# Keys and values of a linear attention: values as weights, both signs' features moving, feature sums on VectorE

## The chip, the cores and the metric

The kernel runs on one core of one Trainium2 chip. The metric is the device time of one execution in microseconds (us). A core has a matrix engine (TensorE, called PE in the profile; its weight loads are PEld), a vector engine (VectorE, DVE), an activation engine (ScalarE, ACT), GpSimd (POOL), and a queue engine (SyncE, SP) that issues most DMA transfers. Matrix products read SBUF, the working memory of 128 partitions, and write PSUM, the accumulation memory of eight banks.

## What is computed

The reference normalizes `x` (2048 tokens, 1024 columns) and feeds it to two parts. One is a linear attention with 32 heads of 32 columns, the other a gated feed-forward of width 3584. The result is `x + attention * silu(feed-forward)`. The attention is what the change touches:

```
phi_k = concat(softmax(k @ w_phi), softmax(-(k @ w_phi)))     # 64 features per token and head
kv  = einsum("bhsf,bhsd->bhfd", phi_k, v)                     # per head: 64 features x 32 value columns, summed over tokens
z   = einsum("bhsf->bhf", phi_k)                              # per head: 64 sums over tokens
num = einsum("bhqf,bhfd->bhqd", phi_q, kv)
den = einsum("bhqf,bhf->bhq", phi_q, z) + 1e-6
o   = num / den
```

So there are 32 features of the positive sign and 32 of the negative for each head, and two sums over the 2048 tokens: `kv` and `z`.

## The kernel before

The large products are made with a Strassen-Winograd scheme of seven block products (the table `ORDER`), in three passes of a split into two 32-bit parts, and each block product is 12 matmuls of 128x128 by 128x512. The stages follow one another: gate and up projections of the feed-forward (about 20 to 1117 us), keys and values (to about 1455), queries (to about 1611), the down projection (to about 2150), and attention output with the output projection (to the end).

In the stage of keys and values `heads` (line 921) runs 16 times: for each half of the heads (`c` 0 and 1, 16 heads each) over eight pairs of token tiles of 128 tokens. One call makes the seven block products (L930), which give keys (already multiplied by `w_phi`) and values of two token tiles. ScalarE and VectorE take them out of PSUM: keys of the first tile after product A12 (L938), values after S2, S1, S3 and S4 (L947 to L955), keys of the second tile after A22.

`keys` (line 898) calls `features` (line 106), which makes the softmax of both signs for one tile: per head the largest and smallest key (L110, L111), the two differences (L112, L113), the exponential on ScalarE (L115), the sums over 32 features (L118), the reciprocal (L119), the product with it (L121). The result is `ev`, 128 tokens by 1024: 512 columns of the positive sign, 512 of the negative. `room_e` (line 889) gives it a place. There are three in turn: two lie in large tiles `rooms_ev` of 2048 columns, where the features have the first 1024, and the values of the tile (`room_v`, line 883) have columns from 1024 on. The third consists of two separate tiles of 512 columns from the pool `work`, tag `h1`, so that its exponential, sums and product are two instructions each.

`kv` (line 902) adds one tile to `kv` and `z` in PSUM. The 512 columns of each sign are taken in groups of four heads: 8 groups `m` by 4 heads `h`, 32 calls. Each call has the 32 features of one head and sign as weights (128 tokens by 32) and moves the head's 32 value columns and two columns of ones (34). So column 32 of the result is `z`. The four heads of a group go to four groups of 32 partitions of the result and to four column groups of the matrix engine. A call on 32-bit data becomes two instructions with two weight loads. `kv_run` (line 912) does this for the two tiles of the previous call of `heads`, between the products S2 and S1 of the present one: 128 instructions of L907. For the last pair, two runs of one tile each are made.

After each half `kv_out` (line 1100) takes the result out: ScalarE copies the `kv` columns, VectorE takes the `z` columns (and adds 1e-6 for the positive sign) into 128x8, PE transposes that (L1111), ScalarE copies it, and SP stores both to DRAM (L1115 to L1118), from where the last stage loads them (`load_z`, `load_kvs`).

In this stage only PE's order is that of the program (`in_order(ENG.PE)`, line 1192). The order on the other engines and queues is set at build time by a planner with estimated durations. In the queries' last part all engines have the program's order again. Operands of `x` (`reload`, line 625) come through the pool `q` of 11 buffers of 512 KB, seven for each pair of tiles; SP issues these loads, the loads of the weights, and the split of `wo` that runs alongside (`wo_split`, line 1181).

Of the kernel before, what the change touches and what calls it, by code (L numbers as in the profile page):

```python
# [8 lines left out]
F = mybir.dt.float32  # L9
# [7 lines left out]
S, D, H, DH, FF = 2048, 1024, 32, 32, 3584  # L17
P = 128
# [10 lines left out]
def tile_kernel(ctx: ExitStack, tc: tile.TileContext, x, wkT, wqT, wv, wphi, wo, w1, w3, w2, out):  # L29
    nc = tc.nc  # L30
    open_pools = {}

    def pool(name, bufs, **kw):

        open_pools[name] = tc.tile_pool(name=name, bufs=bufs, reuse_waits="tile", **kw)
        return open_pools[name].__enter__()
# [47 lines left out]
    z_d = dram.tile([2, 2, 4, 4 * DH], F, name="z_d")  # L84
# [21 lines left out]
    def features(e, whole, p):  # L106

        mm = small.tile([P, 2, 16], F, name="mm2")
        p3 = p.rearrange("p (h f) -> p h f", f=DH)
        nc.vector.tensor_reduce(mm[:, 0, :], p3, axis=AX.X, op=OP.max)  # L110
        nc.vector.tensor_reduce(mm[:, 1, :], p3, axis=AX.X, op=OP.min)  # L111
        nc.vector.tensor_sub(heads_of(e[0]), p3, mm[:, 0, :].unsqueeze(2).to_broadcast([P, 16, DH]))  # L112
        nc.vector.tensor_sub(heads_of(e[1]), mm[:, 1, :].unsqueeze(2).to_broadcast([P, 16, DH]), p3)  # L113
        for part in whole:
            nc.scalar.activation(part, part, AF.Exp)  # L115
        r, n = small.tile([P, H], F, name="r"), H // len(whole)
        for k, part in enumerate(whole):
            nc.vector.tensor_reduce(r[:, n * k:n * k + n], heads_of(part), axis=AX.X, op=OP.add)  # L118
        nc.vector.reciprocal(r, r)  # L119
        for k, part in enumerate(whole):  # L120
            nc.vector.tensor_mul(heads_of(part), heads_of(part), r[:, n * k:n * k + n].unsqueeze(2).to_broadcast([P, n, DH]))  # L121
# [18 lines left out]
    small = pool("small", 2)  # L140
    work = pool("work", 5)
# [5 lines left out]
    ps = pool("ps2", 2, space=PSUM)  # L147
# [25 lines left out]
    def quad(name, dt=R):  # L173
        return qp.tile([P, 2, 4, P], dt, name=name, tag="q")
# [7 lines left out]
    ident = misc.tile([P, P], F, name="ident")  # L182
    consts = misc.tile([P, P], F, name="consts")
# [209 lines left out]
    for tb in range(2):  # L393
        for f in range(NF):
# [11 lines left out]
            first = tb == 0 and f < 2  # L406
# [379 lines left out]
    _, sd = rstd(mvs[0], sds[0], casts)  # L786
# [93 lines left out]
    rooms_ev = [rwp.tile([P, 2048], F, name="ev", tag="rw") for _ in range(2)]  # L880
    rooms_at = [0]

    def room_v(k):
        return rooms_ev[k][:, 1024:1024 + 16 * (DH + 2)].rearrange("p (h d) -> p h d", d=DH + 2)

    for k in range(2):
        nc.gpsimd.memset(room_v(k)[:, :, DH:], 1.0)

    def room_e():
        k = rooms_at[0] % 3  # L890
        rooms_at[0] += 1
        if k < 2:
            e = rooms_ev[k][:, :1024]
            return [e[:, :512], e[:, 512:]], [e]
        e = [work.tile([P, 512], F, name="ev", tag="h1", bufs=2) for _ in range(2)]
        return e, e

    def keys(p, e):
        features(*e, p)
        return e[0]  # L900

    def kv(pkv, first, last, e, v):

        for m in range(8):
            for h in range(4):
                sl = slice(32 * h, 32 * h + 32)
                nc.tensor.matmul(pkv[sl, m], e[m // 4][:, (m % 4) * P + 32 * h:(m % 4) * P + 32 * h + 32],  # L907
                                 v[:, 4 * (m % 4) + h], start=first and m == 0, stop=last, skip_group_check=True)

    pkv, out_now = None, []  # L910

    def kv_run(first, last, tiles):

        nonlocal pkv
        if first:
            pkv = ps.tile([P, 512], F, name="pkv", tag="kv", bufs=1)[:, :8 * (DH + 2)]
            pkv = pkv.rearrange("p (h d) -> p h d", d=DH + 2)
        for n, (e, v) in enumerate(tiles):
            kv(pkv, first and n == 0, last and n + 1 == len(tiles), e, v)

    def heads(first, last, apart, xo, wb, steps, pend):

        bank = {}
        for b, an, bn in ORDER:
            if b not in bank:
                bank[b] = ps.tile([P, 512], F, name=f"bank{b}", tag=f"bk{b}", bufs=BANKS[b])
            n = 0
            for k in range(4):
                for u, w in PASSES:
                    nc.tensor.matmul(bank[b], xo[an][:, u, k], wb[bn][:, w, k], start=an in ("A11", "A12", "S1") and n == 0,  # L930
                                     stop=LAST[b] == an and n == 11, skip_group_check=True)
                    n += 1
            pb, pv = bank[b], bank[b].rearrange("p (h d) -> p h d", d=DH)
            if an == "A11":
                k0 = work.tile([P, 512], F, name="k0", tag="w")
                nc.scalar.copy(k0, pb)
            elif an == "A12":
                nc.vector.tensor_add(k0, pb, k0)  # L938
                e0 = keys(k0, room_e())
            elif an == "S2":  # L940
                if pend:
                    kv_run(*pend)
                    if first:
                        out_now.extend(kv_out(0, pkv))
                v0 = room_v(0)
                d0 = v0[:, :, :DH]
                nc.scalar.copy(d0, pv)  # L947
            elif an == "S1":
                v1 = room_v(1)
                d1 = v1[:, :, :DH]  # L950
                nc.scalar.copy(d1, pv)
            elif an == "S3":
                nc.vector.tensor_add(d1, pv, d1)
            elif an == "S4":
                nc.vector.tensor_add(d0, pv, d0)  # L955
            else:
                if apart:
                    kv_run(first, False, [(e0, v0)])
                    e0 = v0 = d0 = None
                    rooms_ev[0] = None  # L960
                e1 = keys(pb, room_e())
            next(steps)
            if out_now and not first:
                out_now.pop()()
        return (False, last, [(e1, v1)]) if apart else (first, last, [(e0, v0), (e1, v1)])
# [97 lines left out]
    def query_heads(i, first, xo, wb, steps):  # L1063

        bank, rho = {}, small.tile([P, 2, 2, 16], F, name="rho")
        for b, an, bn in ORDER:
# [32 lines left out]

    def kv_out(c, pkv):  # L1100
        kvz = work.tile([P, 512], F, name="kvz", tag="w")
        kva, zt = kvz[:, :8 * DH], kvz[:8, 8 * DH:8 * DH + P]
        zs = small.tile([P, 8], F, name="zs")
        nc.scalar.copy(kva.rearrange("p (m d) -> p m d", d=DH), pkv[:, :, :DH])

        nc.vector.tensor_scalar_add(zs[:, :4], pkv[:, :4, DH], 1e-6)
        nc.vector.tensor_copy(zs[:, 4:], pkv[:, 4:, DH])

        def turned():
            pz = ps.tile([P, 512], F, name="pz", tag="kv", bufs=1)  # L1110
            nc.tensor.transpose(pz[:8, :P], zs, ident)  # L1111
            nc.scalar.copy(zt, pz[:8, :P])

        def store():
            nc.sync.dma_start(kv_d[:, :, :, c].rearrange("j f s m d -> (j f) s (m d)"),  # L1115
                              kva.rearrange("p (s n) -> p s n", s=2))
            for s in range(2):
                nc.sync.dma_start(z_d[s, c], zt[4 * s:4 * s + 4])  # L1118

        return [store, turned]  # L1120

# [55 lines left out]
    ps = pool("ps", 2, space=PSUM)  # L1177
# [16 lines left out]
    for c in range(3):  # L1194
        wbn, last = {}, c == 2
# [257 lines left out]
    old, banks, first, second = None, {}, ready[0], None  # L1453
# [3 lines left out]
    for r, new in enumerate(steps):  # L1457
# [29 lines left out]
        for m, (b, an, bn) in enumerate(TURN):  # L1487
# [30 lines left out]
    ps = pool("ps4", 3, space=PSUM)  # L1518
# [54 lines left out]
    for t in range(NT):  # L1573
        p, last = out_half(t, 0), t + 1 == NT
# [70 lines left out]
```

## Time and profile before

| what | value |
|---|---|
| median of 3 runs | 2367.42 us (2367.08 to 2367.56) |
| the profiled execution's own time | 2366.58 us |
| its span, from first to last instruction | 2364.8 us |
| mean granted clock of TensorE | 0.996 |
| PE, DVE, ACT, POOL busy | 99%, 75%, 38%, 11% of the span |

A row of the timeline gives the start in us from the span's start, the length in us, the engine, the line of the kernel, the operation, `out<-in` by the names of tiles, shapes, how many instructions are merged in the row, and in brackets how long the engine was idle before it and what ended that. A row of grouped instructions ends with busy time and mean duration in ns, then idle time before them. An instruction of PE lasts longer than the distance to the next, since they are pipelined; distances between starts tell what PE is held for.

### The profile page before, as it was taken

Reading aid. Unit: us, or ns where it says so; the run is one execution under the profiler, and the core shown is the slowest. Engines: PE = TensorE matmul, PEld = TensorE weight load, DVE = VectorE, ACT = ScalarE, POOL = GpSimd, SP = SyncE. Lnnn points to the kernel's source line nnn. Section 1 sums busy time; section 2 is a strip of 40 time slices with the busy share of each in tenths; the row PEclk is TensorE's granted clock in tenths of the full one; section 3 lists DMA queues with packets and bytes.
Section 4 is the critical chain, followed back from the end, with each engine's and each line's share of the span. In section 5 each row is a group of like instructions: output and inputs, shape, how many; then the busy total and the mean of one; then the engine's idle time right before and its main releaser. Section 6 shows DMA issues by size and latency. Waiting matters only on the chain.

```text
span 2364.8 us, 37648 instructions
## 1 busy us (share of the span) xinstructions
PE 2338.3 (99%) x14640; PEld 1916.5 (81%) x14640; DVE 1777.7 (75%) x2809; ACT 892.8 (38%) x1575; POOL 256.8 (11%) x213
## 2 busy tenths in 40 slices
PE   8999999999999999999999999999999999999999
PEld 6788877788888888888788888787888888888887
DVE  8877788875688888874566666777678888786775
ACT  6445444443355554443221222334433333352000
POOL 1000000000000000000000000331012222213562
PEclk9999999999999999999999999999999999999999
DMA  3556799997788988875978868986444553479763
GB/s 127 162 190 231 241 312 369 344 310 230 241 273 304 305 293 301 288 259 191 365 275 298 305 231 329 362 299 232 161 134 143 205 178 134 156 248 278 211 178 104
DMA packets 301490, 579.08 MB, mean 245 GB/s; under 512 B 24432, under 2 KB 156672, under 8 KB 298624
## 3 DMA queue, kind: packets, MB, share of 16 engines
q1 hardware_dynamic: 294976, 553.60, 69.3%
q10 hardware_dynamic: 6336, 23.07, 2.5%
q8 instruction: 115, 1.88, 0.3%
q14 instruction: 63, 0.52, 0.1%
HBM read 373.69 MB, written 202.91 MB: 244 GB/s over the span
## 4 chain that ended last, share of the span: by engine, by line
PE 95%; DMA 3%; DVE 1%; ACT 1%; issue 0%; SPq 0%; ACTq 0%
PE bankb L667 25%; PE bankb L1400 13%; PE bankc L667 12%; PE pm L1554 8%; PE bankb L930 7%; PE bankc L1400 6%; PE banka L667 6%; PE bankc L930 3%; PE bankb L1004 3%; PE banka L1400 3%; PE bankc L1004 2%; PE banka L930 2%; PE po L1539 1%; DMA xoA<-xo_d0A 1%; PE pkv L907 1%; PE banka L1004 1%
## 5 line engine op out<-in xcount | busy, mean ns | idle before, releaser
L94 DVE TENSOR_TENSOR bo<-rw,bo 128x512 fp32r<-128x512 f32 x329 | 226.1, 688 | 145.3 <-ACT bo L93 145.1
L1400 PE MATMUL bankb<-bo,as 128*128 128x512 f32 x960 | 236.3, 391 | 0.0
L1400 PEld LDWEIGHTS bankb<-bo,as 128*128 128x128 f32 x960 | 181.1, 189 | 37.7
L93 ACT CAST bo<-rw 128x512 fp32r<-128x512 f32 x329 | 202.3, 618 | 19.3 <-ACT wkvo L93 2.9
L667 PE MATMUL bankb<-op0S,bo 128*128 128x512 f32 x672 | 165.7, 396 | 4.5 <-ACT u L703 2.8
L667 PE MATMUL bankc<-op0S,bo 128*128 128x512 f32 x672 | 162.1, 390 | 0.0
L667 PE MATMUL bankb<-op1S,bo 128*128 128x512 f32 x672 | 161.3, 389 | 0.0
L667 PE MATMUL bankc<-op1S,bo 128*128 128x512 f32 x672 | 161.3, 389 | 0.0
L667 PE MATMUL bankb<-op0A,bo 128*128 128x512 f32 x672 | 159.3, 391 | 1.2 <-ACT op0A L765 0.8
L1554 PE MATMUL pm<-wos,oT 128*128 128x512 f32 x672 | 160.0, 393 | 0.0
L1400 PE MATMUL bankc<-bo,as 128*128 128x512 f32 x624 | 158.4, 389 | 0.0
L667 PE MATMUL bankb<-op1A,bo 128*128 128x512 f32 x672 | 157.9, 390 | 0.0
L667 PEld LDWEIGHTS bankb<-op0S,bo 128*128 128x128 f32 x672 | 125.6, 189 | 37.1 <-issue 5.3
L667 PEld LDWEIGHTS bankb<-op1A,bo 128*128 128x128 f32 x672 | 125.8, 188 | 28.1 <-DVE u L711 2.1
L667 PEld LDWEIGHTS bankb<-op0A,bo 128*128 128x128 f32 x672 | 125.4, 188 | 27.6 <-ACT op0A L765 1.1
L667 PEld LDWEIGHTS bankc<-op0S,bo 128*128 128x128 f32 x672 | 125.6, 188 | 27.3 <-issue 1.2
L667 PEld LDWEIGHTS bankc<-op1S,bo 128*128 128x128 f32 x672 | 126.2, 188 | 26.2
L667 PEld LDWEIGHTS bankb<-op1S,bo 128*128 128x128 f32 x672 | 126.2, 188 | 26.2
L1554 PEld LDWEIGHTS pm<-wos,oT 128*128 128x128 f32 x672 | 124.8, 188 | 27.4 <-DVE oT L1545 0.3
L1400 PEld LDWEIGHTS bankc<-bo,as 128*128 128x128 f32 x624 | 117.2, 188 | 24.4
L1414 DVE TENSOR_TENSOR acc<-bankb,acc 128x512 f32<-128x512 f32 x152 | 102.0, 685 | 32.7 <-PE bankb L1400 32.7
L718 ACT ACTIVATE h<-bankb 128x512 f32<-128x512 f32 x56 | 33.5, 598 | 239.7 <-PE bankb L667 239.5
(290 smaller groups left out, 4305.3 us busy)
## 6 DMA issues: line engine op xcount, KB each, us to landing
rw<-in_w SPq DMA_DIRECT2D x112, 512.0 KB, 4.9
hr<-h_d SPq DMA_DIRECT2D x56, 512.0 KB, 4.7
h_d<-h SPq DMA_DIRECT2D x108, 256.0 KB, 5.6
xoS<-xo_d0S SPq DMA_DIRECT2D x44, 512.0 KB, 7.2
xoS<-xo_d1S SPq DMA_DIRECT2D x44, 512.0 KB, 6.7
xoA<-xo_d0A SPq DMA_DIRECT2D x33, 512.0 KB, 5.3
xoA<-xo_d1A SPq DMA_DIRECT2D x33, 512.0 KB, 5.3
e_d<-eq ACTq DMA_DIRECT2D x32, 512.0 KB, 6.5
```

Of the source, the lines that this page charges most:

```text
L93: nc.scalar.copy(hi, src)
L94: (by or nc.vector).tensor_sub(lo, src, hi.bitcast(F))
L667: nc.tensor.matmul(bank[b], bos[tb, f][bn][:, w, k], ao[an][:, u, k], start=first and n == 0, stop=LAST[b] == an and n == 11, skip_group_c ...
L718: nc.scalar.activation(h1, bank["b"], AF.Silu)
L907: nc.tensor.matmul(pkv[sl, m], e[m // 4][:, (m % 4) * P + 32 * h:(m % 4) * P + 32 * h + 32], v[:, 4 * (m % 4) + h], start=first and m == 0 ...
L930: nc.tensor.matmul(bank[b], xo[an][:, u, k], wb[bn][:, w, k], start=an in ("A11", "A12", "S1") and n == 0, stop=LAST[b] == an and n == 11, ...
L1004: nc.tensor.matmul(bank[b], xo[an][:, u, k], wb[bn][:, w, k], start=an in ("A11", "A12", "S1") and n == 0, stop=LAST[b] == an and n == 11, ...
L1400: nc.tensor.matmul(bank[b], t[:, u, pos + k], bos[kb, bn, k][:, w], start=first and n == 0, stop=LAST[b] == an and n == 5, skip_group_chec ...
L1414: nc.vector.tensor_add(c, pb, c)
L1539: nc.tensor.matmul(po[32 * j:32 * j + 32, a, 64 * k:64 * k + 64], kvs[sl, j, c, k], et[sl, :, 4 * k + j], start=True, stop=True, skip_grou ...
L1554: nc.tensor.matmul(p, oTs[t, h][:, a, k], wos[c, 4 * h + k][:, b], start=n == 0, stop=n == 3 * ND - 1)
```

## The change

Weights and moving data of the small products change places. Per head one call now has the 32 value columns as weights and moves the head's 64 features, both signs at once; so a tile takes 16 calls. The result of a head has values on the partitions, and two block transposes on VectorE in `kv_out` turn it. The columns of ones next to the values go. `z` is formed on VectorE: `z_add`, called in `kv_run` for every tile, adds the tile's 1024 features to a running sum of two tiles of 128x512 (the first tile's features are kept in place and added with the second's). At the end of each half, four matmuls with a 128x32 matrix of ones, 256 columns each, sum it over the 128 partitions, and VectorE takes the result out of PSUM. Those two running sums take the two `work` tiles of tag `h1`, and the third place for features becomes a tile of the pool `q`, held for the stage and as wide as the other two. `z` is stored by four small transfers in place of two.

```
     def room_v(k):
-        return rooms_ev[k][:, 1024:1024 + 16 * (DH + 2)].rearrange("p (h d) -> p h d", d=DH + 2)
-
-    for k in range(2):
-        nc.gpsimd.memset(room_v(k)[:, :, DH:], 1.0)
+        return rooms_ev[k][:, 1024:1536].rearrange("p (h d) -> p h d", d=DH)
+
+    ones = consts[:, 64:96]
+    nc.gpsimd.memset(ones, 1.0)
 
     def room_e():
         k = rooms_at[0] % 3
         rooms_at[0] += 1
-        if k < 2:
-            e = rooms_ev[k][:, :1024]
-            return [e[:, :512], e[:, 512:]], [e]
-        e = [work.tile([P, 512], F, name="ev", tag="h1", bufs=2) for _ in range(2)]
-        return e, e
+        if k == len(rooms_ev):
+            rooms_ev.append(quad("ev", F).rearrange("p u k t -> p (u k t)"))
+        e = rooms_ev[k][:, :1024]
+        return [e[:, :512], e[:, 512:]], [e]
...
     def kv(pkv, first, last, e, v):
 
-        for m in range(8):
+        e = e.rearrange("p (s h f) -> p s h f", s=2, f=DH)
+        for m in range(4):
             for h in range(4):
                 sl = slice(32 * h, 32 * h + 32)
-                nc.tensor.matmul(pkv[sl, m], e[m // 4][:, (m % 4) * P + 32 * h:(m % 4) * P + 32 * h + 32],
-                                 v[:, 4 * (m % 4) + h], start=first and m == 0, stop=last, skip_group_check=True)
+                nc.tensor.matmul(pkv[sl, m], v[:, 4 * m + h], e[:, :, 4 * m + h],
+                                 start=first and m == 0, stop=last, skip_group_check=True)
+
+    zsum = []
+
+    def z_add(e):
+
+        if not zsum:
+            zsum.append(e)
+            return
+        if len(zsum) == 1:
+            zsum.extend(work.tile([P, 512], F, name="zsum", tag="h1", bufs=2) for _ in range(2))
+        for n in range(2):
+            half = slice(512 * n, 512 * n + 512)
+            nc.vector.tensor_add(zsum[1 + n], zsum[0][:, half] if zsum[0] is not None else zsum[1 + n], e[:, half])
+        zsum[0] = None
...
         for n, (e, v) in enumerate(tiles):
+            z_add(e)
             kv(pkv, first and n == 0, last and n + 1 == len(tiles), e, v)
...
     def kv_out(c, pkv):
         kvz = work.tile([P, 512], F, name="kvz", tag="w")
-        kva, zt = kvz[:, :8 * DH], kvz[:8, 8 * DH:8 * DH + P]
-        zs = small.tile([P, 8], F, name="zs")
-        nc.scalar.copy(kva.rearrange("p (m d) -> p m d", d=DH), pkv[:, :, :DH])
-
-        nc.vector.tensor_scalar_add(zs[:, :4], pkv[:, :4, DH], 1e-6)
-        nc.vector.tensor_copy(zs[:, 4:], pkv[:, 4:, DH])
+        kva, zt, zs = kvz[:, :8 * DH], kvz[:, 8 * DH:], zsum[1:]
+        zsum.clear()
+        for n in range(2):
+            nc.vector.transpose(kva[:, P * n:P * n + P].rearrange("p (m d) -> p m d", d=DH), pkv[:, :, DH * n:DH * n + DH])
 
         def turned():
             pz = ps.tile([P, 512], F, name="pz", tag="kv", bufs=1)
-            nc.tensor.transpose(pz[:8, :P], zs, ident)
-            nc.scalar.copy(zt, pz[:8, :P])
+            for n in range(4):
+                nc.tensor.matmul(pz[32 * n:32 * n + 32, :256], ones, zs[n // 2][:, n % 2 * 256:n % 2 * 256 + 256],
+                                 start=True, stop=True, skip_group_check=True)
+            nc.vector.tensor_scalar_add(zt[:64], pz[:64, :256], 1e-6)
+            nc.vector.tensor_copy(zt[64:], pz[64:, :256])
```

More of the change, by code (lines that the diff above doesn't have):

```diff
@@ L915, in kv_run @@
         if first:
-            pkv = ps.tile([P, 512], F, name="pkv", tag="kv", bufs=1)[:, :8 * (DH + 2)]
-            pkv = pkv.rearrange("p (h d) -> p h d", d=DH + 2)
+            pkv = ps.tile([P, 512], F, name="pkv", tag="kv", bufs=1)[:, :512 // 2]
+            pkv = pkv.rearrange("p (m n) -> p m n", m=4)
+            zsum.clear()
         for n, (e, v) in enumerate(tiles):
+            z_add(e)
             kv(pkv, first and n == 0, last and n + 1 == len(tiles), e, v)
@@ L945, in heads @@
                 v0 = room_v(0)
-                d0 = v0[:, :, :DH]
+                d0 = v0
                 nc.scalar.copy(d0, pv)
@@ L949, in heads @@
                 v1 = room_v(1)
-                d1 = v1[:, :, :DH]
+                d1 = v1
                 nc.scalar.copy(d1, pv)
@@ L1101, in kv_out @@
         kvz = work.tile([P, 512], F, name="kvz", tag="w")
-        kva, zt = kvz[:, :8 * DH], kvz[:8, 8 * DH:8 * DH + P]
-        zs = small.tile([P, 8], F, name="zs")
-        nc.scalar.copy(kva.rearrange("p (m d) -> p m d", d=DH), pkv[:, :, :DH])
-        nc.vector.tensor_scalar_add(zs[:, :4], pkv[:, :4, DH], 1e-6)
-        nc.vector.tensor_copy(zs[:, 4:], pkv[:, 4:, DH])
+        kva, zt, zs = kvz[:, :8 * DH], kvz[:, 8 * DH:], zsum[1:]
+        zsum.clear()
+        for n in range(2):
+            nc.vector.transpose(kva[:, P * n:P * n + P].rearrange("p (m d) -> p m d", d=DH), pkv[:, :, DH * n:DH * n + DH])
         def turned():
             pz = ps.tile([P, 512], F, name="pz", tag="kv", bufs=1)
-            nc.tensor.transpose(pz[:8, :P], zs, ident)
-            nc.scalar.copy(zt, pz[:8, :P])
+            for n in range(4):
[3 more added lines that the diff above has]
+            nc.vector.tensor_copy(zt[64:], pz[64:, :256])
         def store():
@@ L1116, in store @@
                               kva.rearrange("p (s n) -> p s n", s=2))
-            for s in range(2):
-                nc.sync.dma_start(z_d[s, c], zt[4 * s:4 * s + 4])
+            for n in range(4):
+                nc.sync.dma_start(z_d[n // 2, c].rearrange("(a g) n -> a (g n)", a=2)[n % 2:n % 2 + 1], zt[32 * n:32 * n + 1])
         return [store, turned]
```

2 lines of the change are left out of this document (1 added, 1 removed).

## The prediction

> **What bounds the kernel now.** I read the page first: its busy lines and the chain by engine.
>
> ```profile
> span 2364.8 us, 37648 instructions
> PE 2338.3 (99%) x14640; PEld 1916.5 (81%) x14640; DVE 1777.7 (75%) x2809; ACT 892.8 (38%) x1575; POOL 256.8 (11%) x213
> PE 95%; DMA 3%; DVE 1%; ACT 1%; issue 0%; SPq 0%; ACTq 0%
> ```
>
> TensorE (PE) is busy for 99% of the span and is 95% of the chain that ended last. The edit sits in the key and value stage, so the windows view of that stage comes next.
>
> ```profile
> core 0: us, PE busy (x) PEld busy (x) DVE busy (x) ACT busy (x) POOL busy (x), PEclk, DMA share, GB/s
> 1139.25:1453.00 313.75, 312.80 (x3184) 256.99 (x3185) 196.31 (x293) 66.87 (x103) 0.00 (x0) 0.99 0.81 288
> ```
>
> PE idles 0.95 us of 313.75 there and VectorE (DVE) is busy 196.31, or 63%. GpSimd is not used. So a microsecond is gained or lost here by what PE itself executes, or by a wait that does not exist today. One period of PE, from the timeline of PE alone:
>
> ```profile
> 1360.48 1.37 PE L907 MATMUL pkv<-ev 128*32 128x34 f32 x128
> 1361.78 3.02 PE L930 MATMUL bankc<-op3T,xoS 128*128 128x512 f32 x12
> 1372.80 2.88 PE L930 MATMUL bankb<-op3B,xoA 128*128 128x512 f32 x12
> 1375.52 2.88 PE L930 MATMUL banka<-op3B,xoA 128*128 128x512 f32 x12
> 1378.24 2.88 PE L930 MATMUL bankb<-op3T,xoS 128*128 128x512 f32 x12
> 1381.05 1.34 PE L907 MATMUL pkv<-ev 128*32 128x34 f32 x128
> 1382.40 3.00 PE L930 MATMUL bankc<-op3T,xoS 128*128 128x512 f32 x12
> ```
>
> A product starts every 2.72 us (1372.80, 1375.52, 1378.24). The run of 128 small matmuls on L907 holds PE from its first start to the next product's: 1.30 us at 1360.48 and 1.35 us at 1381.05. I use 1.30. The next fence's first row counts 2048 such instructions: 15 full runs and two half runs, where the last pair of tiles is taken apart. The whole target of the change is therefore about 15 x 1.30 + 2 x 0.70 = 21 us.
>
> **The change part by part.**
>
> *The small matmuls.* Before, each of 16 heads' features made two 34-column products per tile (32 calls); now it is one 64-column product per head (16 calls). Every call is two instructions, so a full run goes from 128 to 64 instructions, and each of the four 32-column groups from 32 of 34 columns to 16 of 64. The half run shows what count costs, the others what columns cost (the rows of the line, then timelines; the row after a run is the next product):
>
> ```profile
> L907 PE MATMUL pkv<-ev x2048: 191/197/220, 1153.1 to 1467.5; 128*32 128x34 f32 x187
> 1455.17 0.77 PE L907 MATMUL pkv<-ev 128*32 128x34 f32 x64
> 1455.87 3.01 PE L1004 MATMUL bankb<-op4B,xoA 128*128 128x512 f32 x12
> 2030.03 0.59 PE L1324 MATMUL us<-early_z,consts 128*128 128x256 f32 x2
> L1324 PE MATMUL us<-early_z,consts x2: 377/377/377, 2030.0 to 2030.2; 128*128 128x256 f32 x2
> 2188.84 0.86 PE L1539 MATMUL po<-acc,kvs 64*32 64x64 f32 x64
> 2189.63 1.66 PE L1554 MATMUL pm<-wos,oT 128*128 128x512 f32 x6
> ```
>
> - 64 instructions of 34 columns hold PE 0.70 us, 128 hold it 1.30 us: 0.60 us per 64, or 37.5 ns for each instruction of one column group, and 0.10 us that does not depend on the count.
> - Two instructions of 256 columns take 0.59 us where one takes 0.377, so they start 0.213 us apart: 0.83 ns a column. At that rate 34 columns are 28.3 ns and 64 are 53.3 ns. So 37.5 is 28.3 of columns and 9.2 of something per instruction.
> - New run: 16 x 53.3 = 0.85 us at least, 16 x 62.5 = 1.00 us if the 9.2 stays; with the 0.10, between 0.95 and 1.10. I take **1.03**, a gain of 0.27 per full run; 0.14 per half run likewise (0.70 to 0.56). Sum: 15 x 0.27 + 2 x 0.14 = **4.3 us**.
> - Wider ends, kept for the range: if time goes with columns alone (1024 against 1088), the run is 1.20 x 0.94 + 0.10 = 1.23, a gain of 1.1 us in all. If it goes with the count alone, it is 0.70, and the half run 0.40: 15 x 0.60 + 2 x 0.30 = 9.6 us. The attention rows (64 instructions of 64 columns, 0.79 us) lie near that end, but they use half the rows each and so eight places of the array, not four.
>
> The Trainium skill, in "TensorEngine Tiling (Array Packing)", section Performance Considerations, says that a small matmul carries about 60 cycles of overhead, so that one column costs as much as 60. By that, 34 and 64 columns cost nearly the same and the run goes with the count, 0.70 us. The rows above only half agree, because 9.2 ns of 37.5 go with the instruction; what that rule would give is the second rival.
>
> *The sums of the features.* The ones columns of the values go; instead DVE adds each tile to a running sum, two additions of 128x512 a tile, 30 for each half of the heads, 60 in all. The rows by group give the price, and the waits of DVE in the stage the room:
>
> ```profile
> L130 DVE TENSOR_TENSOR wkv<-wkv 128x512 f32<-128x512 f32 x8 | 5.5, 685 | 0.0
> L118 DVE TENSOR_REDUCE r<-ev 128x32 f32<-128x1024 f32 x20 | 24.4, 1220 | 26.0 <-ACT ev L115 26.0
> L955 DVE TENSOR_TENSOR ev<-bankc,ev 128x512 f32<-128x512 f32 x15 | 10.4, 692 | 28.8 <-PE bankc L930 28.8
> L110 DVE TENSOR_REDUCE mm<-bankb 128x16 f32<-128x512 f32 x15 | 10.4, 692 | 35.8 <-PE bankb L930 35.8
> L953 DVE TENSOR_TENSOR ev<-bankb,ev 128x512 f32<-128x512 f32 x15 | 10.4, 691 | 18.4 <-PE bankb L930 18.4
> ```
>
> 60 x 0.685 = 41 us of DVE. DVE's idle time in the stage is 313.75 - 196.31 = 117 us, in pieces of 1.2 to 2.4 us (28.8/15, 35.8/15, 18.4/15, 26.0/20). Four additions a period need 2.7 us, and a period has 7.7 us of idle. The additions read only what DVE wrote, so none waits for another engine, and nothing waits for a sum before the end of the stage. I cost them at **0**, covered by that idle time; without the cover, each addition ahead of a critical step costs up to 0.6 us (third rival).
>
> *The last sums.* Per half of the heads, PE's transpose of eight columns becomes four matmuls with a matrix of ones, 256 columns each, side by side in the column groups. The nearest row is the folding of the weights, also 256 columns twice through one place:
>
> ```profile
> 1310.81 2.88 PE L930 MATMUL bankb<-op3B,xoA 128*128 128x512 f32 x12
> 1313.53 0.27 PE L1111 MATMUL pz<-ident,zs 128*8 128x128 f32 x1
> 1313.56 3.01 PE L930 MATMUL banka<-op3B,xoA 128*128 128x512 f32 x12
> 1316.40 2.88 PE L930 MATMUL bankb<-op3T,xoS 128*128 128x512 f32 x12
> 121.51 0.40 PE L543 MATMUL banka<-wf,early_z 32*32 32x256 f32 x1
> 122.16 2.11 PE L667 MATMUL bankc<-op0S,bo 128*128 128x512 f32 x8
> ```
>
> Now: 1310.81 to 1313.56 to 1316.40 is 5.59 against 2 x 2.72, so 0.15 us. Folding holds PE for 0.65 us, and entry and exit of such a run cost 0.1 to 0.2 more, as 2.81 (1378.24 to 1381.05) and 2.84 (1313.56 to 1316.40) stand to 2.72. So 0.8 - 0.15 = 0.65 more, twice: **1.3 us lost** (0.8 to 1.6).
>
> *Moved off PE's path, cost 0.* The copy of the sums goes from ScalarE to DVE, two block transposes are added (DVE's for 128x256 take 0.41 us), and two more small stores go through SP: under 2 us of DVE per half, twice, covered by the same idle. The third feature room is now one tile of 1024, so its work becomes two instructions fewer on DVE and one on ScalarE. Its space is one of the 11 buffers of x operands. Of those, seven are in use and four ahead; with one fewer, a load starts one product (2.72 us) later.
>
> ```profile
> xoS<-xo_d0S SPq DMA_DIRECT2D x44, 512.0 KB, 7.2
> ```
>
> Ten products (27 us) of lead less 7.2 us to land leave 20 us; one product less leaves 17. Loads queued behind on SP move by as much, and nothing on PE waits for them.
>
> **Sum:** -4.3 + 1.3 = **-3.0 us**. The profiled execution took 2366.58 us (its span 2364.8 and 1.8 around it), 0.84 under the median of 2367.42. -3.0 gives 2363.6 for it, and **2364.4** by the median.
>
> **The rivals.**
>
> *Second: time goes with the count.* The run takes 0.70, as the half run does with as many instructions: -9.6 + 1.3 = -8.3, **2359.1**. For it: 0.60 us per 64 instructions, and the 0.79 of the attention rows. Against it: the four column groups must pass 16 x 64 columns each, 0.85 us at the rate of L1324.
>
> *Third, the slower side: the additions land in the second tile's chain.* DVE's order is the planner's, not the program's. The chain from that tile's exponential to its matmuls is tight:
>
> ```profile
> 1210.02 1.06 ACT L115 ACTIVATE ev<-ev 128x1024 f32<-128x1024 f32 x1
> 1211.12 1.22 DVE L118 TENSOR_REDUCE r<-ev 128x32 f32<-128x1024 f32 x1 [1.82 <-ACT ev L115]
> 1212.26 0.69 DVE L938 TENSOR_TENSOR k<-banka,k 128x512 f32<-128x512 f32 x1
> 1213.67 1.21 DVE L121 TENSOR_TENSOR ev<-ev,r 128x1024 f32<-128x1024 f32 x1
> 1214.87 1.29 PEld L907 LDWEIGHTS pkv<-ev 128*32 128x32 f32 x128 [0.35 <-issue]
> ```
>
> L121 ends at 1214.88, when the run begins. Only because the first tile goes first (0.60 us) does PE not wait; with the shorter run that cover is about 0.45. Behind a PE that waits there stand all later products. It decides at 0.45 us: two additions (1.2 us) between L118 and L121 stall 0.75 us, 15 times, 11.3 - 3.0 = +8.3, **2375.7**. One costs 0.15 x 15 = 2.3 and leaves 2366.7. Against it: the 1.82 us of idle before L118 takes two additions for nothing, and the ones in question are ready a period earlier.
>
> *Fourth: the gain is given back.* At the entry to the next stage PE waits (waits view, and windows of the wait and what follows):
>
> ```profile
> PE bankb L1400 <- DVE af L94: 3.4, 1, 3.4
> 1617.38:1621.20 3.82, 0.40 (x2) 0.00 (x1) 3.75 (x9) 1.68 (x3) 0.00 (x0) 0.80 1.03 419
> 1621.20:1626.50 5.30, 5.30 (x13) 4.19 (x14) 3.73 (x9) 3.02 (x6) 0.00 (x0) 0.50 0.84 268
> ```
>
> If what ends it does not come earlier with PE, the wait grows by 3.0 and nothing is left: **2367.4**. Against it: the DMA of the stage is at 1.03 of its share there, but its loads take room that PE frees, so they should move along. The same rows hold a lever: after this idle the granted clock is 0.50 for 5.3 us, which costs half of that, 2.65 us, and a shorter wait would save it. The Trainium skill, "TensorE: Matmul & The Clock Gate", Part 1, says that an idle window of about 3.4 us halves the clock; the trace agrees (3.4 us of wait, then 0.50). By that rule a small shift either way could turn 2.65 us.
>
> **How the numbers follow.** About 0.2% (4.7 us) is what a measurement of this kernel tells from no change: below 2362.7 is faster, above 2372.2 slower.
>
> - Forecast, 2364.4, own range 2361.5 to 2367: 0.49, of it 0.06 under 2362.7.
> - Second, 2359.1: 0.24.
> - Third, 2375.7: 0.15.
> - Fourth, 2367.4 (with 2.65 to either side): 0.12, of it 0.01 above 2372.2.
>
> Faster 0.30, same 0.54, slower 0.16. The range takes in the second rival and most of the way to the third: 2358.5 to 2374.
>
> **What would show it.** From the first L907 start to the next product: 1.03 us forecast; 0.70 is the second rival, 1.23 or more says that columns are all. The period falls from 20.6 to 20.3 us. PE's idle time in the stage stays near 1 us; a DVE wait on L907's line is the third rival, and the wait at L1400 grown to 6 us the fourth. The matmuls with ones hold PE 0.65 us, twice. DVE's busy time in the stage rises by 35 to 45 us. What would make the prediction wrong: a column rate other than 0.83 ns in column groups, or a planner's order that puts the additions ahead of features.

## The result, and the profile after

The changed kernel takes **2379.15 us** (median of 5 runs, 2378.62 to 2381.25) against 2367.42 for the kernel before in the same comparison (5 runs, 2364.78 to 2369.08). The ratio is 1.0057, with a 95% interval of 1.0046 to 1.0068. It is slower by 11.7 us, where 3.0 us of gain were forecast.

The span of the profiled execution went from 2364.8 to 2376.5 us. The page of the changed kernel, its span, busy line and chain by engine:

```profile
span 2376.5 us, 35643 instructions
PE 2349.6 (99%) x13630; PEld 1910.5 (80%) x13630; DVE 1811.4 (76%) x2853; ACT 891.0 (37%) x1561; POOL 258.0 (11%) x212
...
PE 90%; DMA 4%; DVE 4%; ACT 1%; issue 0%; POOL 0%; ACTq 0%; SPq 0%; POOLq 0%
```

TensorE (PE) runs about a thousand instructions fewer and is busy 11.3 us longer (2349.6 against 2338.3). The loss is therefore not in the main a wait: PE is slower at work that it already had.

**The stage that was changed.** The timeline of PE alone in the changed kernel, one period of the stage (the key and value products are on L946 now), then a run that a wait splits into two halves, and the matmuls with ones:

```profile
1363.44 1.10 PE L907 MATMUL pkv<-ev 128*32 128x64 f32 x64
...
1383.86 1.10 PE L907 MATMUL pkv<-ev 128*32 128x64 f32 x64
1384.89 3.01 PE L946 MATMUL bankc<-op3T,xoS 128*128 128x512 f32 x12
```

```profile
1176.43 0.65 PE L907 MATMUL pkv<-ev 128*32 128x64 f32 x32
1178.32 0.65 PE L907 MATMUL pkv<-ev 128*32 128x64 f32 x32 [1.23 <-DVE ev L121]
1178.90 3.03 PE L946 MATMUL bankc<-op2T,xoS 128*128 128x512 f32 x12
```

```profile
1313.57 2.88 PE L946 MATMUL bankb<-op3B,xoA 128*128 128x512 f32 x12
1316.38 0.64 PE L1126 MATMUL pz<-zsum,consts 128*32 128x256 f32 x8
1316.95 3.02 PE L946 MATMUL banka<-op3B,xoA 128*128 128x512 f32 x12
1319.81 2.43 PE L946 MATMUL bankb<-op3T,xoS 128*128 128x512 f32 x10
```

The full run holds PE from 1383.86 to 1384.89, 1.03 us, as forecast. Half a run takes 0.58 (1178.32 to 1178.90), and the period is 20.42 us (1363.44 to 1383.86) where it was 20.57 and 20.3 were forecast. The matmuls with ones cost 0.80 us beside two products (1313.57 to 1319.81 is 6.24, less 2 x 2.72), which is 0.65 more than the transpose of before, again as forecast. Two waits are new, 1.2 us on L121 and 1.3 on L969; one of the kernel before, 0.9 us on ScalarE's eviction L951, is gone. The waits view of PE:

```profile
PE bankb L1417 <- DVE af L94: 3.4, 1, 3.4
PE bankb L946 <- DMA xoA<-xo_d0A: 3.4, 1, 3.4
...
PE bankb L946 <- DVE ev L969: 1.3, 2, 0.7
PE pkv L907 <- DVE ev L121: 1.2, 1, 1.2
```

**The stages that were not changed.** The down projection (L1400 before, L1417 after) shows what the stage does not. The rows are those of the line's view: duration of one matmul in ns, lowest, median and highest, then the first and the last start in us. First before, then after:

```profile
L1400 PE MATMUL bankc<-bo,as x624: 388/389/398, 1615.4 to 2150.0; 128*128 128x512 f32 x156
L1400 PE MATMUL bankc<-late,as x48: 389/389/390, 1698.2 to 1766.0; 128*128 128x512 f32 x48
```

```profile
L1417 PE MATMUL bankc<-bo,as x624: 387/392/398, 1618.1 to 2160.6; 128*128 128x512 f32 x156
L1417 PE MATMUL bankc<-late,as x48: 388/392/398, 1702.0 to 1771.0; 128*128 128x512 f32 x48
```

The same 624 matmuls stretch over 542.5 us instead of 534.6. The loss inside this stage alone is 7.9 us, though the diff has no line in it. The second row of each fence is a handy gauge for the rest of the document, and I call it the **late stretch**: from the first to the last start of bankc<-late,as it is 67.8 us before and 69.0 after. Matched in order between the two traces, the start-to-start distances of the 9,840 matmuls with 512 columns are 14.0 us longer in sum (those below 260 ns counted, so that waits stay out). In the stretch from 1660 to 2000 us the mean distance is 226.7 ns before and 230.2 after. The lengthening repeats in a fixed pattern from period to period, and e2_shift below, another kernel with the same shift, has the same sum of 14.0 us, so it is not noise.

What could reach all stages? The change took the tile `zs` away. It was 8 columns of 4 bytes in a pool with two buffers, so 64 bytes of each partition. SBUF is filled from both ends here: most pools grow from the left, and the others are declared with `side="right"`. All tiles that stand behind `zs` on the left moved down by 64 bytes, and those on the right stayed. (Some also took another buffer of their pool, a multiple of 2,048 bytes away.) By the addresses in the built programs, each moving tile and its weight tile lay a multiple of 512 bytes apart before, for all 9,840 matmuls. In 2,640 of them the moving tile is on the right and the weights on the left, and for these the distance is now off by 64. The longer start-to-start distances stand at these matmuls and next to them: 7.4 us of the 14.0 at the 2,640 themselves, 6.5 within twelve matmuls of one of them, and 0.1 at the other 4,594 that were counted. The stage of queries, where no tile's distance to its weights is off, is not longer. The groups of the first stage show it. In both kernels, op0S lies on the left like its weights, and part of op1A lies on the right. Before, and after:

```profile
L667 PE MATMUL bankc<-op0S,bo 128*128 128x512 f32 x672 | 162.1, 390 | 0.0
L667 PE MATMUL bankb<-op1A,bo 128*128 128x512 f32 x672 | 157.9, 390 | 0.0
```

```profile
L667 PE MATMUL bankc<-op0S,bo 128*128 128x512 f32 x672 | 162.1, 390 | 0.0
L667 PE MATMUL bankb<-op1A,bo 128*128 128x512 f32 x672 | 159.1, 392 | 0.0
```

### The profile page after: what moved, and what is told of

Its sections match the earlier page's. It is cut to its first block, busy times and chain, and to the rows that moved or that the text cites. A ratio compares the mean times of both kernels' runs of the same rounds, so it can differ in the third digit from the quotient of the medians.

```text
span 2376.5 us, 35643 instructions
## 1 busy us (share of the span) xinstructions
PE 2349.6 (99%) x13630; PEld 1910.5 (80%) x13630; DVE 1811.4 (76%) x2853; ACT 891.0 (37%) x1561; POOL 258.0 (11%) x212
## 4 chain that ended last, share of the span: by engine, by line
PE 90%; DMA 4%; DVE 4%; ACT 1%; issue 0%; POOL 0%; ACTq 0%; SPq 0%; POOLq 0%
PE bankb L667 25%; PE bankb L1417 13%; PE bankc L667 12%; PE pm L1571 8%; PE bankb L946 6%; PE bankc L1417 6%; PE banka L667 6%; PE banka L1417 3%; PE bankc L946 3%; PE banka L946 1%; PE bankb L1020 1%; PE po L1556 1%; DMA xoA<-xo_d0A 1%; DMA wo_raw<-in_wo 1%; PE bankc L1020 1%; DVE r L998 1%
## 5 line engine op out<-in xcount | busy, mean ns | idle before, releaser
L1417 PE MATMUL bankb<-bo,as 128*128 128x512 f32 x960 | 239.6, 394 | 0.0
L1417 PEld LDWEIGHTS bankb<-bo,as 128*128 128x128 f32 x960 | 181.1, 189 | 41.0
L989 POOL TENSOR_TENSOR eq<-q,mm 128x512 f32<-128x512 f32 x24 | 25.2, 1050 | 1528.3 <-DVE mm L987 1507.8
L1417 PE MATMUL bankc<-bo,as 128*128 128x512 f32 x624 | 160.4, 392 | 0.0
L1417 PEld LDWEIGHTS bankc<-bo,as 128*128 128x128 f32 x624 | 117.2, 188 | 26.3
```

The lines of the kernel that those rows point to most:

```text
L989: eng.tensor_sub(e[:, 0], p3, mm[:, 0, :].unsqueeze(2).to_broadcast([P, 16, DH]))
L1417: nc.tensor.matmul(bank[b], t[:, u, pos + k], bos[kb, bn, k][:, w], start=first and n == 0, stop=LAST[b] == an and n == 5, skip_group_chec ...
```

## The experiments

The **theory**: the 64 bytes cost most of the loss, because of where the operands lie (8 to 10 us of it were expected). The **rival**: the new instructions cause the loss (additions on VectorE, the third room), by delays that go on into later stages. Times are medians, and each ratio is against the kernel before in the same comparison (2366.51, 2366.37 and 2365.48 us in the three sets, of 27, 21 and 27 runs).

### The 64 bytes put back, and taken away alone

e1_pad is the changed kernel with a dummy tile of the size of `zs`:

```diff
+        nc.gpsimd.memset(small.tile([P, 8], F, name="zs"), 0.0)
```

> The changed kernel with a dummy tile of 128x8 (2 buffers, 64 bytes a partition) kept in the small pool, at the place where the removed tile zs had been; otherwise unchanged. Theory (placement): the change took 64 bytes out of the small pool, all tiles behind it moved by 64 bytes, and matmuls all over the kernel became up to 1.5% slower, 8 to 9 us outside the stage; with the tile back the drift outside the stage is gone and the time is 2369 to 2371 us. Rival (the loss is made in the stage, by waits, and by what PE executes): 2378 to 2380 us, and the distance between matmuls in the down projection stays at 230 ns against 226.7 before.

e2_shift is the kernel before, with the same instructions, but with `zs` placed in unused columns of a tile that exists already:

```diff
-        zs = small.tile([P, 8], F, name="zs")
+        zs = kvz[:, 8 * DH + P:8 * DH + P + 8]
```

> The kernel before with its zs put into unused columns of kvz, so that the small pool is 64 bytes shorter, and with not one instruction more or less. Placement theory: 2375 to 2377 us, with the drift of the changed kernel outside the stage (matmuls of the down projection 230 ns apart). Rival: 2367 us, 226.7 ns apart.

Measured: e1_pad 2365.29 us (2363.24 to 2368.92, 11 runs), ratio 0.9995 [0.9986, 1.0004]; e2_shift 2380.80 us (2377.71 to 2383.00, 5 runs), ratio 1.0061 [1.0047, 1.0075]. The late stretch of e1_pad, then of e2_shift:

```profile
L1418 PE MATMUL bankc<-late,as x48: 388/390/390, 1696.1 to 1763.9; 128*128 128x512 f32 x48
```

```profile
L1400 PE MATMUL bankc<-late,as x48: 388/392/398, 1701.1 to 1770.1; 128*128 128x512 f32 x48
```

With the padding it is 67.8 us again, and without any of the new instructions but with the shift it is 69.0. Both directions agree: the shift alone costs 14.3 us by the medians, and putting it back takes 13.9 off (2379.15 to 2365.29, from two comparisons). That is more than I had expected of either (2369 to 2371 us and 2375 to 2377), because I had priced the placement by the stretch outside the stage alone. The rival is out as the cause of the loss. That the change without the shift is faster than before is not shown by e1_pad, whose interval takes in 1.

### What about the place matters

Two readings are left: each tile's own address counts, or the distance between the moving tile and the weights. In none of the five kernels here does the order of the instructions change against the changed kernel. e5_right leaves the left side where the change put it, and moves the right side by the same 64 bytes:

```diff
-    edge[1].tile([P, 120], F, name="edge_r")
+    edge[1].tile([P, 136], F, name="edge_r")
```

> The changed kernel with 64 bytes more padding taken away on the other side: the pools of the right side of SBUF move 64 bytes down too, so that every distance between a tile of the left side and one of the right is as in the kernel before, and only the addresses themselves are 64 bytes lower. If what counts is the distance between a weight tile and a moving tile, the 128x512 matmuls come back to 226.7 ns from start to start in the down projection and the time to 2365 to 2367 us. If what counts is where each tile lies by itself (its address against some multiple), they stay at 230 ns or more and the time at 2377 to 2383 us.

The other four move the left side of the changed kernel by other amounts, through the padding behind one tile. X is -16, +32, +80 and +144 columns, which puts the left side at -128, +64, +256 and +512 bytes against the kernel before:

```diff
-    early_z = small.tile([P, 256 + PAD], F, name="early_z", bufs=1)[:, :256]
+    early_z = small.tile([P, 256 + PAD + X], F, name="early_z", bufs=1)[:, :256]
```

> The changed kernel with 64 bytes less in the padding tile early_z: the left side's tiles lie 128 bytes lower than in the kernel before, 64 lower than in the changed one. If the cost comes back with every 128 bytes (64 bytes is then half a period), the matmuls come back to 226.7 ns and the time to 2365 to 2367 us. If it grows with the shift or has a longer period, the time is 2377 us or more.

> The changed kernel with 128 bytes more in early_z: the left side's tiles lie 64 bytes higher than in the kernel before. By a period of 128 bytes this is the same case as the changed kernel: 230 ns and 2377 to 2381 us. If the kernel before sits at one best place of a longer period, or if only lower addresses cost, the time is anything from 2365 to 2385 us, and the spacing of the matmuls tells which.

> The changed kernel with 320 bytes more in early_z: the left side lies 256 bytes higher against the right side than in the kernel before. In the kernel before every moving tile and every weight tile lie a multiple of 512 bytes apart; 64 and 128 bytes off were both slow. If a multiple of 256 is enough, the matmuls whose moving tile lies on the right and whose weights lie on the left come back to 226.7 ns and the time to 2365 to 2367 us; if the distance has to be a multiple of 512, they stay at 229 to 232 ns and the time at 2377 to 2384 us.

> The changed kernel with 576 bytes more in early_z: the left side lies 512 bytes higher than in the kernel before. If the distance counts by multiples of 512 bytes (or of a divisor of it), 226.7 ns and 2365 to 2367 us; if the kernel before sat at one single good place, or the period is 1024 or more, about 2380 us as with the other shifts.

The late stretch of e5_right, e6_m128, e8_p64, e9_p256 and e10_p512, one fence each in this order:

```profile
L1417 PE MATMUL bankc<-late,as x48: 389/389/389, 1697.1 to 1764.9; 128*128 128x512 f32 x48
```

```profile
L1417 PE MATMUL bankc<-late,as x48: 387/394/398, 1702.3 to 1771.4; 128*128 128x512 f32 x48
```

```profile
L1417 PE MATMUL bankc<-late,as x48: 394/394/394, 1700.4 to 1769.8; 128*128 128x512 f32 x48
```

```profile
L1417 PE MATMUL bankc<-late,as x48: 389/389/389, 1695.4 to 1763.1; 128*128 128x512 f32 x48
```

```profile
L1417 PE MATMUL bankc<-late,as x48: 389/389/389, 1692.5 to 1760.3; 128*128 128x512 f32 x48
```

| kernel | left side, bytes | left against right, bytes | late stretch, us | median, us | ratio |
|---|---|---|---|---|---|
| after | -64 | -64 | 69.0 | 2379.15 | 1.0057 [1.0046, 1.0068] |
| e2_shift | -64 | -64 | 69.0 | 2380.80 | 1.0061 [1.0047, 1.0075] |
| e1_pad | 0 | 0 | 67.8 | 2365.29 | 0.9995 [0.9986, 1.0004] |
| e5_right | -64 | 0 | 67.8 | 2366.47 | 1.0000 [0.9991, 1.0008] |
| e6_m128 | -128 | -128 | 69.1 | 2380.34 | 1.0058 [1.0046, 1.0071] |
| e8_p64 | +64 | +64 | 69.4 | 2383.51 | 1.0068 [1.0056, 1.0081] |
| e9_p256 | +256 | +256 | 67.7 | 2363.91 | 0.9990 [0.9981, 0.9999] |
| e10_p512 | +512 | +512 | 67.8 | 2363.80 | 0.9990 [0.9981, 0.9999] |

e5_right decides: every left tile lies 64 bytes lower than before, and the cost is gone, because the right side went along. What counts is the distance between the sides, and the matmuls that are slower are those that reach from one side to the other, with their neighbours. At 0, 256 and 512 bytes off the matmuls keep their pace; at -128, -64 and +64 they lose it, and e2_shift, e6_m128 and e8_p64 are 14 to 17 us over the kernel before. In e8_p64 every matmul of the row takes 394 ns; in e1_pad none takes more than 390. A multiple of 256 bytes is enough for this kernel, and 128 is not. Whether 32 or 192 bytes off would cost as much wasn't tried.

The four kernels that keep the distance and have the additions on VectorE also show what the change is worth without the shift: 1.2 us less than before (e1_pad), 0.1 more (e5_right), 1.6 less (e9_p256) and 1.7 less (e10_p512). The last two have intervals that leave out 1, though barely.

### The additions on VectorE

e4_noadd is e1_pad with the running additions left out; only the first two tiles of each half are still added, so its sums lack the other tiles:

```diff
-            nc.vector.tensor_add(zsum[1 + n], ...)
+            if zsum[0] is not None:
+                nc.vector.tensor_add(zsum[1 + n], zsum[0][:, half], e[:, half])
```

> e1_pad without the running additions: only the first two tiles of each half are added, 4 additions in place of 60 (the sums z, and so the output, lack the other tiles). Theory (additions lie in VectorE's idle time): 0 to 1.3 us under e1_pad, the 1.3 us being two waits on line L969. Rival (the additions delay the features): 4 us or more under e1_pad.

Measured: 2363.37 us (2361.48 to 2365.62, 11 runs), ratio 0.9987 [0.9978, 0.9995]. By the medians that is 1.9 us under e1_pad in the same comparison, more than the 0 to 1.3 of my theory and less than the 4 of its rival, though the two intervals overlap. PE's waits in the stage, e1_pad and then e4_noadd:

```profile
PE bankb L946 <- DMA xoA<-xo_d0A: 3.5, 1, 3.5
PE pkv L907 <- DVE ev L121: 1.3, 1, 1.3
PE bankb L946 <- DVE ev L969: 0.8, 2, 0.5
```

```profile
PE bankb L947 <- DMA xoA<-xo_d0A: 3.1, 1, 3.1
PE pkv L907 <- DVE ev L121: 1.3, 1, 1.3
```

The wait on L969, VectorE's eviction of a product into a room, comes from the additions: 0.8 us in this execution. Every kernel here with the additions on VectorE has it, with 0.6 to 1.6 us, and no kernel without them. The wait on L121 does not come from them. The rest of the 1.9 has no wait to it, and may be scatter between executions.

e7_pool keeps the additions and gives them to GpSimd, which has little to do in this stage (e1_pad, with one word changed):

```diff
-            nc.vector.tensor_add(zsum[1 + n], ...)
+            nc.gpsimd.tensor_add(zsum[1 + n], ...)
```

> The changed kernel with the padding put back (as in e1_pad, 2365.3 us) and its running additions on GpSimd instead of VectorE. If the 1.9 us by which the run without the additions was shorter is VectorE's time (they stand between the evictions that TensorE waits for), this one comes to about 2363.4 us, 1.9 below e1_pad, and the waits of the product on VectorE's evictions go. The rival: GpSimd's additions are long or share VectorE's access to SBUF, and the time is that of e1_pad or up to 5 us more, with VectorE's own instructions in the stage longer than in e1_pad.

Measured: 2363.36 us (2360.47 to 2366.41, 11 runs), ratio 0.9985 [0.9976, 0.9994]. It is as fast as the kernel without the additions and faster than before by 3.0 us, in an interval that leaves out 1. The views of three lines follow: the additions in e7_pool, then two operations of VectorE, L113 with two inputs in SBUF and L111 with one, in e7_pool and in e1_pad. The three durations are the shortest, the median and the longest in ns:

```profile
L921 POOL TENSOR_TENSOR zsum<-zsum,ev x56: 1277/1292/1745, 1168.5 to 1458.3; 128x512 f32<-128x512 f32 x56
```

```profile
L113 DVE TENSOR_TENSOR ev<-mm,k x16: 677/1776/1778, 1127.1 to 1439.9; 128x512 f32<-128x512 f32 x16
L111 DVE TENSOR_REDUCE mm<-k x16: 629/679/679, 1125.9 to 1437.8; 128x16 f32<-128x512 f32 x16
```

```profile
L113 DVE TENSOR_TENSOR ev<-mm,k x16: 683/685/687, 1128.8 to 1443.6; 128x512 f32<-128x512 f32 x16
L111 DVE TENSOR_REDUCE mm<-k x16: 629/679/680, 1127.6 to 1442.4; 128x16 f32<-128x512 f32 x16
```

An addition takes 1.29 us on GpSimd (0.68 on VectorE), and VectorE's operation with two inputs in SBUF takes 1776 ns beside it instead of 685: the 13 of these that run at the same time as an addition take 1771 ns or more. L111, which has one input, stays at 679, though 14 of its 16 run beside an addition for part of their time. The rival's mechanism is real, then, but it falls on operations that have time to spare. The Trainium skill, "SBUF — State Buffer", section Who interferes with whom, says that the two engines share a pair of ports, which one of them holds for a whole instruction; the trace agrees, with 1776 against 685 ns.

### The third room

The other new wait of PE, on L121, comes once, at the first tile of the second pair. That tile's features start late: L112 follows L111 at once in the kernel before, and stands 9 us behind it after. VectorE's timeline, before and after:

```profile
1153.06 0.68 DVE L111 TENSOR_REDUCE mm<-k 128x16 f32<-128x512 f32 x1
1153.65 0.68 DVE L112 TENSOR_TENSOR ev<-k,mm 128x512 f32<-128x512 f32 x1
```

```profile
1157.28 0.68 DVE L111 TENSOR_REDUCE mm<-k 128x16 f32<-128x512 f32 x1
...
1165.61 0.69 DVE L971 TENSOR_TENSOR ev<-bankc,ev 128x512 f32<-128x512 f32 x1 [1.96 <-PE bankc L946]
1166.22 0.68 DVE L112 TENSOR_TENSOR ev<-k,mm 128x512 f32<-128x512 f32 x1
```

My reading was that this room, now one of the 11 buffers of x operands, is not free in time. e3_early (e1_pad) was to take it ahead of the stage's first loads:

```diff
+    rooms_ev.append(quad("ev", F).rearrange("p u k t -> p (u k t)"))
...
-        if k == len(rooms_ev):
-            rooms_ev.append(quad("ev", F).rearrange("p u k t -> p (u k t)"))
```

> e1_pad with the third place for features taken from the pool q before the stage's first loads, not at its first use. Theory (the one-time wait of 1.2 us for the features at the second run of small matmuls comes from a place that is free only after the loads ahead of it in the pool): 1.0 to 1.5 us under e1_pad, with no wait of PE on line L907. Rival (the loads of x that then start later make PE wait instead): as e1_pad or up to 3 us above it.

e11_both joins it to e7_pool:

> The running additions on GpSimd and the padding back (as e7_pool, 2363.4 us) and the third room taken before the stage's first loads (as e3_early, which was the same as e1_pad). If VectorE's lateness behind the additions is what made e3_early lose its early start again, the early start now stays and this comes to 2362 us; if the wait for the third tile's features (1.3 us) is not a matter of the room, it is that of e7_pool within 0.5 us.

Measured: e3_early 2365.27 us (2362.77 to 2368.79, 11 runs), ratio 0.9996 [0.9987, 1.0005]; e11_both 2362.76 us (2359.67 to 2367.67, 11 runs), ratio 0.9986 [0.9976, 0.9995]. PE's waits in the stage, e3_early and then e11_both:

```profile
PE bankb L945 <- DMA xoA<-xo_d0A: 4.1, 2, 3.2
PE bankc L945 <- ACT ev L966: 1.8, 2, 1.6
PE bankb L945 <- DVE ev L968: 1.6, 3, 0.7
PE pkv L906 <- DVE ev L121: 1.3, 1, 1.3
```

```profile
PE bankb L945 <- DMA xoA<-xo_d0A: 3.2, 1, 3.2
PE pkv L906 <- DVE ev L121: 1.3, 1, 1.3
```

The wait of 1.3 us is there in both, but they don't test my reading. The moved line left the built program as it was: e3_early has the instructions, addresses and semaphores of e1_pad, and e11_both those of e7_pool. So each of the two programs was measured twice, with 2365.29 and 2365.27 us, and 2363.36 and 2362.76 (3.0 and 2.7 under the kernel before). The other waits also tell how much one program's executions differ: 0.8 us on VectorE and none on ScalarE in e1_pad, 1.6 and 1.8 in e3_early. The best version measured is that of e7_pool.

What the built program shows speaks for the room. It lies in a buffer of x operands that the first pair's own product S1 still reads. In the changed kernel that product starts at 1157.05 us, and the next one at 1159.92:

```profile
1157.05 3.04 PE L946 MATMUL bankc<-op2T,xoS 128*128 128x512 f32 x12
1159.92 2.93 PE L946 MATMUL bankb<-op2T,xoS 128*128 128x512 f32 x12
```

So L112, which writes into the room, can't come before about 1159.9 us; behind L111 it could have come at 1157.9. From there to 1166.22 it is VectorE's order, fixed when the program is built, that keeps L112 behind the evictions L969 and L971, while VectorE idles 4.39 us before the one and 1.96 before the other. Whether a room that is free earlier would move L112 forward in that order and end the wait was not tried, and the cause of the wait stays open.

## Why the prediction was wrong

- **The step that failed** is in the first part: "So a microsecond is gained or lost here by what PE itself executes, or by a wait that does not exist today." The sum -4.3 + 1.3 took the rest of the kernel as unmoved. The diff's removed line `zs = small.tile([P, 8], F, name="zs")` was costed as an operand of the transpose. It was an allocation too, and its 64 bytes put 2,640 matmuls of the first stage, the changed one, the down projection and the output off the distance at which they run at full pace. e1_pad and e2_shift price that at about 14 us. No rival had it; the third came nearest in time (2375.7) with another mechanism.
- **The small matmuls: right.** 1.03 us forecast, 1.03 measured, and the second rival (0.70) and the wider end (1.23) are out. That it agrees to the hundredth is luck in part: 1.03 was the middle between two cases, and half a run took 0.58 where 0.56 were forecast. By these two, eight instructions of a column group take 0.45 us, or 56 ns each (53.3 and 62.5 were the cases), and 0.13 us does not go with their number (0.10 was taken). The rate of 0.83 ns a column fits this, but is not shown apart from what an instruction costs by itself.
- **The matmuls with ones: right.** 0.65 us more, twice.
- **The additions at 0: too low.** Their cover was not whole. The kernel without them is 1.9 us faster by the medians, 0.8 of it seen as a wait. The third rival's kind of delay occurred at another place (L969, not between L118 and L121) and twice in the stage, not 15 times. VectorE's busy time in the stretch looked at rose by 28.4 us (196.31 to 224.73, the third busy time in the windows row below, over the same stretch as before), less than the forecast 35 to 45. The stretch ends before the last additions, but up to 1475 us, behind them, it is 30.9 (208.92 to 239.82).

```profile
1139.25:1453.00 313.75, 308.83 (x2221) 250.05 (x2222) 224.73 (x330) 65.44 (x91) 0.00 (x0) 0.99 0.83 285
```

- **PE's idle time, forecast to stay near 1 us:** it is 4.92 in this row (313.75 less 308.83). Of that, 3.0 is the wait for `xoA`, which ended just ahead of the stretch in the kernel before, at 1139.25 us, and ends at 1142.27 now; the rest is the new waits.
- **The moved things at 0: nearly.** The third room was priced by the loads that start later, and PE's wait for them is 3.4 us where it was 3.2. When the room itself gets free was not asked, and the one wait of 1.2 us on L121 is at its first tile. That the room causes it is argued above, not shown.
- **Giving the gain back (the fourth rival): no.** The wait at the entry of the down projection is 3.4 us before and after.
- **The sum: right only where these two costs are out of the way.** Without the shift, the gain is between none and 1.7 us (e1_pad, e5_right, e9_p256, e10_p512); with the additions on GpSimd as well it is 2.7 to 3.0 us, the forecast size. The first term is seen by itself: the period is 20.29 us in e1_pad, and 20.3 were forecast. That the rest is the same gain, term by term, is an inference: 4.3 of shorter runs less 1.3 of ones less the wait of 1.2 would be 1.8, and the scatter of the medians is of the size of the rest.

## What to carry to other kernels

In a kernel whose tiles are stacked as here, an edit that adds or drops a tile moves all tiles behind it, so look at what the allocator does with the others before costing the instructions; a dummy tile of the same size separates the two effects in one run. If TensorE gets slower in stages that the diff doesn't touch, compare the start-to-start distance of the same matmuls in both traces, and sort them by where their operands lie. Where weights and moving data come from pools at opposite ends of SBUF, try padding so that the distance stays a multiple of 256 bytes, as it had to here. And before an experiment without effect is read as an answer, look whether its edit changed the built program at all.

## What the runs showed of the hardware

In this kernel the pace of a 128x512 matmul depends on the distance in SBUF between its moving tile and its weights. In the stretch from 1660 to 2000 us they start 226.7 ns apart on average where the shift of the left side against the right is 0, 256 or 512 bytes, and 230.1 to 230.8 ns apart where it is 64 or 128. That is 1.5 to 1.8% more, a mean over matmuls that are hit and others that are not. At -64 about half of the 14.0 us stands at the neighbours of those matmuls; at +64 (e8_p64) it is 16.0 of 19.9 us at the matmuls themselves. The Trainium skill, "SBUF — State Buffer", section SBUF: two separate sides, says that TensorE never waits for anyone at SBUF, and "TensorE: Matmul & The Clock Gate", section Part 2: What happens when you issue a matmul, that loading the next weights takes no bandwidth from the running matmul. Read together, they let one expect that the place of a tile costs nothing. At -64, +64 and -128 bytes the measurement says otherwise, in e2_shift with the same instructions as before. Which part of the chip causes it, no run shows, nor whether a matmul's own weights count or those loaded for the next, since all weights lie on the left.
